# Loading the first half of an output projection in two transfers instead of one

## The chip, the core and the metric

The kernel runs on one core of a Trainium2 chip. A core has TensorE (matrix products), VectorE, ScalarE and GpSimd, which compute, and SyncE, which here issues most of the transfers. Sixteen DMA engines move data between HBM and the on-chip memory (SBUF); results of TensorE go to PSUM. The metric is the device time of one execution in microseconds (us), lower is better. The times given are of three timed runs; the profile is of one further execution.

## The reference

One token (a vector x of 1024) goes through two branches, and the results are added to it. A is attention with 32 query heads and 4 key/value heads over the last 4096 positions of a cache; B is a two-layer network with 3584 hidden units. Everything is bf16.

```python
xn = layernorm(x)
# A: attention over the last W = 4096 cached positions
q = (layernorm(x) @ wq)                      # 1024 -> 32 heads x 128
p = softmax(q k^T * 128**-0.5)               # 8 query heads share one k/v head
A = (p v).reshape(4096) @ wo                 # 4096 -> 1024
# B: network on the layernorm of xn
B = gelu(layernorm(xn) @ w1 + b1) @ w2 + b2  # 1024 -> 3584 -> 1024
out = x + A + B
```

The inputs that are read once each: the two cache windows k and v (4 MB each), wq (8 MB), w1 and w2 (7 MB each), wo (8 MB), together 39.9 MB.

## The kernel before, in words

All large inputs pass through a ring of four SBUF buffers of 32 KB in each of 128 partitions (`ring_tile`). They are loaded by SyncE in this order: k (four loads), wq in two halves, w1 in two halves, v (three loads), w2 in two halves, wo in two halves. A load into the ring waits until the buffer's earlier content has been used. The two halves of wo take the buffers of the second half of w1 and of v, so the first half of wo waits for the last matmul on w1 (L250), and the second half for the last matmul of the attention's weighted sum (`o_all`, L306). A DMA announces its landing on one of eight semaphores that are used in turn; a load on a semaphore waits for the landing of the load that used it before.

A weight matrix is laid out so that partition p holds a run of consecutive rows. For wo (4096 x 1024) that is 32 rows of 2 KB per partition, 16 in each half; "row r" below is such a slice of 128 partitions x 1024 numbers. The first half came in one load of 16 rows, a contiguous 32 KB run per partition. The second half comes in loads of 8, 4, 2, 1 and 1 rows (list `cuts`, L219).

The last stage is a product of vectors with matrices. The list `chunk_src` holds the 28 rows of w2 (kind "h", multiplied with the hidden vector `hT`) and then the 32 rows of wo (kind "o", multiplied with the attention output `o8`), in that order. For each row TensorE does two matmuls of 512 columns, one for each half of the 1024 outputs, in two column groups of the array, and adds them in PSUM in `accf` (L327). A matmul waits for the load that brought its row. The last four rows (TAIL) are split otherwise: at L331 and L332 the sum so far is copied out to `bulk`, and the last four rows go to two other PSUM tiles `acct` of 320 and 192 columns (L343). Between the second and third of them the copied sum of the 192 columns is added by a matmul with the identity (L339). VectorE then adds the 320 columns (L347), ScalarE copies the 192 (L348), and two small DMAs write the output.

TensorE runs its instructions in program order: the rows of w2, the rows of wo, then the tail.

Of the kernel before, what the change touches and what calls it, by code (L numbers as in the profile page):

```python
# [16 lines left out]
def kernel(  # L17
# [45 lines left out]
    def ring_tile(name):  # L63
        return ring.tile([P, RING_ELEMS], BF16, tag="ring", name=name, align_bytes=256)
# [151 lines left out]
        nc.sync.dma_start(out=tv, in_=w2_v[:, nr * i:nr * (i + 1), :])  # L216
        chunk_src += [("h", nr * i + r, tv[:, r, :]) for r in range(nr)]
    wo_v = A_wo.rearrange("(p c) n -> p c n", p=P)
    for i, cuts in enumerate([[0, 16], [0, 8, 12, 14, 15, 16]]):  # L219
        nr = CWO // 2  # L220
        t = ring_tile(f"wo{i}")
        tv = t[:].rearrange("p (r n) -> p r n", r=nr)
        for a, b in zip(cuts[:-1], cuts[1:]):
            nc.sync.dma_start(out=tv[:, a:b, :], in_=wo_v[:, nr * i + a:nr * i + b, :])
        chunk_src += [("o", nr * i + r, tv[:, r, :]) for r in range(nr)]
# [156 lines left out]
```

## Time and profile before

| | |
|---|---|
| three timed runs, median | 101.91 us (101.83 to 101.96) |
| profiled execution, its own time | 102.12 us |
| span of the profiled execution | 100.3 us |
| TensorE busy | 45.9 us (46%) |
| VectorE, ScalarE, GpSimd busy | 38.2, 30.0, 8.2 us |
| moved by DMA | 39.91 MB, 398 GB/s over the span |
| mean granted clock of TensorE | 0.912 |
| SyncE's queue: packets, share of 16 DMA engines' time | 2866, 93.6% |

The span goes from the first to the last instruction of the program; the time also has what lies around it. In the profile, L327 is line 327 of the kernel; "PE" is TensorE's matmuls. A line of the page with a digit for each of 40 slices gives the busy share of a slice in tenths, and "PEclk" the granted share of TensorE's clock. "From issue to landing" of a DMA counts its wait in the queue behind other loads. An arrow in the table of groups names the instruction or load that ended an idle stretch.

### The profile page before, as it was taken

What the parts mean: (1) busy time and instruction counts of PE and PEld (TensorE: products, weight loads), DVE (VectorE), ACT (ScalarE), POOL (GpSimd) and SP (SyncE); (2) the same over time, 40 slices, a digit from 0 to 9 for tenths busy, and PEclk for the clock granted to TensorE, in tenths of its full rate; (3) what the DMA queues carried; (4) which work ended last, traced back from release to release, by engine and by line L of the source; (5) the groups of instructions that cost most, each with busy time, mean ns of one, the idle gap of its engine ahead of it and who ended that gap; (6) DMA issues with size and microseconds to landing.
All of it is one profiled execution on the core that took longest, in us unless ns stands there. A gap on an engine that the chain in (4) does not pass through costs nothing.

```text
span 100.3 us, 917 instructions
## 1 busy us (share of the span) xinstructions
PE 45.9 (46%) x361; PEld 17.6 (18%) x361; DVE 38.2 (38%) x26; ACT 30.0 (30%) x35; POOL 8.2 (8%) x38
## 2 busy tenths in 40 slices
PE   0005230008500940590078721999376910299990
PEld 0002200002100300230033311344132400033330
DVE  0079999999999960000001235600600000000030
ACT  5206500007999999800000029200040000000010
POOL 7901560000000000000000001000000000000000
PEclk9999999999999999999655998599999999655998
DMA  4899999999999998998999998998999999999910
GB/s 52 372 428 427 503 470 418 457 431 418 418 418 392 469 446 366 503 400 372 413 428 421 438 510 377 492 423 372 503 400 415 418 418 431 425 421 410 399 37 1
DMA packets 2951, 39.91 MB, mean 398 GB/s; under 512 B 370, under 2 KB 388, under 8 KB 772
## 3 DMA queue, kind: packets, MB, share of 16 engines
q1 hardware_dynamic: 2866, 39.85, 93.6%
q8 instruction: 3, 0.05, 0.2%
q10 hardware_dynamic: 82, 0.01, 0.1%
HBM read 39.86 MB, written 0.00 MB: 397 GB/s over the span
## 4 chain that ended last, share of the span: by engine, by line
DMA 79%; PE 17%; DVE 0%; SPq 0%; issue 0%
DMA wo<-in_A_wo_dram 33%; DMA w<-in_B_w_dram 24%; DMA wq<-in_A_wq_dram 17%; PE accf L327 9%; DMA k_sb<-in_A_k_cache_dram 5%; PE accq L233 4%; PE acch L250 3%; PE acct L343 1%; DVE res L347 0%; PE acct L339 0%; SPq L202 0%
## 5 line engine op out<-in xcount | busy, mean ns | idle before, releaser
L195 ACT COPY kT<-kt_scr 32x4096 bf16<-32x4096 bf16 x5 | 18.0, 3601 | 10.4 <-DVE kt_scr L186 10.3
L186 DVE STREAM_TRANSPOSE kt_scr<-k_sb 128x4096 bf16<-128x4096 bf16 x4 | 17.4, 4414 | 5.7 <-DMA k_sb<-in_A_k_cache_dram 5.7
L233 PE MATMUL accq<-wq,xnT 128*1 128x512 bf16 x64 | 7.2, 626 | 15.6 <-DMA wq<-in_A_wq_dram 15.6
L197 DVE COPY kT<-kt_scr 32x4096 bf16<-32x4096 bf16 x11 | 13.4, 1218 | 0.2
L327 PE MATMUL accf<-wo,o 128*1 128x512 bf16 x56 | 9.0, 498 | 6.5 <-DMA wo<-in_A_wo_dram 6.5
L250 PE MATMUL acch<-w,yT 128*1 128x448 bf16 x64 | 6.3, 572 | 10.9 <-DMA w<-in_B_w_dram 10.9
L332 DVE COPY bulk<-accf 33x320 f32<-33x320 f32 x1 | 0.5, 483 | 23.7 <-ACT bulk L331 23.7
L306 PE MATMUL o_all<-v_sb,eTb 128*32 128x512 bf16 x32 | 8.6, 435 | 1.1 <-DVE rs L290 1.1
L259 DVE COPY qm_f<-qT_ps 128x16 bf16<-128x16 bf16 x2 | 0.3, 169 | 17.9 <-PE qT_ps L254 17.9
L331 ACT COPY bulk<-accf 33x192 f32<-33x192 f32 x1 | 0.3, 313 | 22.1 <-PE accf L327 22.1
L327 PE MATMUL accf<-w,hT 128*1 128x512 bf16 x56 | 6.4, 379 | 0.9 <-DMA w<-in_B_w_dram 0.9
L233 PEld LDWEIGHTS <-xnT 128*1 128x1 bf16 x64 | 2.1, 115 | 20.6 <-issue 19.8
L276 ACT COPY m_rep<-m_row 1x128 f32<-1x128 f32 x1 | 0.3, 297 | 16.7 <-DVE m_row L274 16.7
L327 PEld LDWEIGHTS <-o 128*1 128x1 bf16 x56 | 3.0, 104 | 12.5 <-issue 10.8
L250 PEld LDWEIGHTS <-yT 128*1 128x1 bf16 x64 | 2.1, 115 | 14.7 <-issue 14.7
L306 PEld LDWEIGHTS <-eTb 128*32 128x32 bf16 x32 | 3.4, 109 | 5.8 <-issue 1.9
L297 POOL TENSOR_SCALAR zcol<-l_loc 128x1 f32<-128x1 f32 x1 | 0.2, 238 | 46.4 <-ACT e L283 46.4
L134 PE MATMUL x_ps<-x,spread 32*128 32x8 bf16 x4 | 0.2, 163 | 7.8 <-DMA x<-in_A_x_dram 7.8
L327 PEld LDWEIGHTS <-hT 128*1 128x1 bf16 x56 | 2.4, 83 | 4.4 <-issue 1.2
L313 ACT CAST o_bf<-o_f 32x128 bf16<-32x128 f32 x1 | 0.3, 297 | 9.4 <-DVE o_f L311 9.4
L309 DVE TENSOR_TENSOR o_m<-o_all,grs 32x512 f32<-32x512 f32 x1 | 0.7, 678 | 5.9 <-PE o_all L306 5.9
L145 PE MATMUL ln_tot<-st,ones_f 128*128 128x2 f32 x4 | 1.2, 363 | 2.8 <-ACT sq L143 2.8
(81 smaller groups left out, 39.9 us busy)
## 6 DMA issues: line engine op xcount, KB each, us to landing
w<-in_B_w_dram SPq DMA_DIRECT2D x4, 3584.0 KB, 19.2
wq<-in_A_wq_dram SPq DMA_DIRECT2D x2, 4096.0 KB, 24.0
k_sb<-in_A_k_cache_dram SPq DMA_DIRECT2D x4, 1024.0 KB, 9.1
wo<-in_A_wo_dram SPq DMA_DIRECT2D x1, 4096.0 KB, 33.2
v_sb<-in_A_v_cache_dram SPq DMA_DIRECT2D x1, 2048.0 KB, 19.4
v_sb<-in_A_v_cache_dram SPq DMA_DIRECT2D x2, 1024.0 KB
wo<-in_A_wo_dram SPq DMA_DIRECT2D x1, 2048.0 KB, 20.9
wo<-in_A_wo_dram SPq DMA_DIRECT2D x1, 1024.0 KB, 23.0
```

What stands on the lines that cost most here:

```text
L145: nc.tensor.matmul(tot[:], lhsT=ones_f[:], rhs=st[:], start=True, stop=True)
L186: nc.vector.transpose(out=scr[:, g, :], in_=k2[:, g, :])
L195: nc.scalar.copy(out=dst, in_=src)
L197: nc.vector.tensor_copy(out=dst, in_=src)
L233: nc.tensor.matmul(accq[32 * t:32 * t + 1, b, :], lhsT=xnT[:, c:c + 1], rhs=w3[:, r, j * 512:(j + 1) * 512], start=(c == 0), stop=(c == C ...
L250: nc.tensor.matmul(acch[32 * t:32 * t + 1, b, :NH], lhsT=yT[:, c:c + 1], rhs=w3[:, r, j * NH:(j + 1) * NH], start=False, stop=(c == C - 1) ...
L259: nc.vector.tensor_copy(out=dst, in_=src)
L306: nc.tensor.matmul(o_all[:].rearrange("h g d -> h (g d)"), lhsT=eTb[:, 32 * c:32 * c + 32], rhs=v4[:, :, c, :], start=(c == 0), stop=(c == ...
L309: nc.vector.tensor_tensor(out=o_m[:], in0=o_all[:], in1=grs[:].unsqueeze(2).to_broadcast([Hq, Hkv, Dh]), op=ALU.mult)
L327: nc.tensor.matmul(accf[32 * half:32 * half + 1, :], lhsT=vec[kind](c), rhs=wap[:, half * 512:(half + 1) * 512], start=False, stop=(idx == ...
L332: nc.vector.tensor_copy(out=bulk[0][:], in_=accf[0:33, 0:N1])
L343: nc.tensor.matmul(t[32 * half:32 * half + 1, :], lhsT=vec[kind](c), rhs=wap[:, half * 512 + n0:half * 512 + n1], start=(idx == 0), stop=( ...
```

## The change

The list of row bounds for the first half of wo gets one more bound, 8. The loop over neighbouring bounds then issues two loads of eight rows (16 KB per partition) in place of one of sixteen (32 KB per partition), into the same buffer, one behind the other. Every other load, and each instruction of the compute engines, stays. The matmuls on rows 0 to 7 wait for the first load, those on rows 8 to 15 for the second. The loads that come after it use the next semaphore in turn.

```diff
     wo_v = A_wo.rearrange("(p c) n -> p c n", p=P)
-    for i, cuts in enumerate([[0, 16], [0, 8, 12, 14, 15, 16]]):
+    for i, cuts in enumerate([[0, 8, 16], [0, 8, 12, 14, 15, 16]]):
         nr = CWO // 2
         t = ring_tile(f"wo{i}")
         tv = t[:].rearrange("p (r n) -> p r n", r=nr)
         for a, b in zip(cuts[:-1], cuts[1:]):
             nc.sync.dma_start(out=tv[:, a:b, :], in_=wo_v[:, nr * i + a:nr * i + b, :])
         chunk_src += [("o", nr * i + r, tv[:, r, :]) for r in range(nr)]
```

## The prediction

> **What bounds the kernel now.** I read the page first for the slices over time, then the DMA issues, the chain that ended last, and last a table of stretches cut where the granted clock changes. The page's slices:
>
> ```profile
> PE   0005230008500940590078721999376910299990
> PEclk9999999999999999999655998599999999655998
> DMA  4899999999999998998999998998999999999910
> wo<-in_A_wo_dram SPq DMA_DIRECT2D x1, 4096.0 KB, 33.2
> ...
> wo<-in_A_wo_dram SPq DMA_DIRECT2D x1, 2048.0 KB, 20.9
> wo<-in_A_wo_dram SPq DMA_DIRECT2D x1, 1024.0 KB, 23.0
> ```
>
> One slice is 2.51 us. The transfers are busy from the second slice to the 38th without a hole, so loading 39.9 MB sets the length, and whatever changes only in the middle is free. The long landings (33.2 us for the first half of wo) are queueing behind earlier loads. After the 38th slice only a tail is left, and there TensorE matters. The chain that ended last:
>
> ```profile
> 53.95 33.17 DMA wo<-in_A_wo_dram
> ...
> 87.16 8.98 PE accf L327 x54
> 96.14 0.44 PE acct L343 x7
> 96.57 0.46 PE acct L339 x4
> 97.03 0.47 PE acct L343 x6
> ...
> 97.53 0.48 DVE res L347
> ```
>
> The first half of wo lands whole at 87.12. From there TensorE works without a pause to 97.5, since a backlog (16 rows) lies before it and the other half arrives meanwhile. By the landing records of the trace the later pieces arrive at 91.96 (8 rows), 94.40 (4), 95.63 (2), 96.23 and 96.85 (1 each). The last row's matmuls start at 97.18, 0.33 us after their data. So the tail of this execution is TensorE's, but with only 0.33 us over the last landing.
>
> Stretches of TensorE, cut at the trace's clock changes (the columns after the stretch and its length are busy time, granted clock, DMA share, GB/s):
>
> ```profile
> 55.26:58.67 3.41, 1.99 (x33) 1.00 1.08 458
> 58.67:62.09 3.42, 0.60 (x4) 1.00 1.10 473
> 62.09:65.50 3.41, 3.04 (x8) 0.50 0.97 420
> 79.15:82.56 3.41, 1.53 (x16) 1.00 1.07 461
> 82.56:85.98 3.42, 0.00 (x0) 1.00 0.98 422
> 85.98:89.39 3.41, 2.23 (x12) 0.50 0.97 418
> 89.39:92.81 3.42, 3.42 (x20) 0.50 0.96 405
> 92.81:96.22 3.41, 3.41 (x38) 1.00 0.77 305
> ```
>
> Every change of clock lies on a grid of 3.413 us, and the busy time of the stretch before it decides. At full clock, stretches with 1.53 and 1.99 us of work kept it, and those with 0.60 and 0.00 lost it. At half clock, 2.23 did not bring it back, while 3.04 and 3.42 did. So the idle time before 87.16 costs the clock, and the unbroken backlog that follows wins it back at 92.81, in time for the tail. This is the row on which the forecast turns. A pair of matmuls (one row of wo) takes 0.427 us at half clock and 0.2155 at full clock, by the starts of L327.
>
> **The change part by part.**
>
> *One load becomes two: the queue.* SP issues one more load at about 54.3 us. That takes 0.33 to 0.43 us of SP, which then waits until 71.06 for o_all to free the ring buffer of the next load: hidden by 16 us. The loads share eight semaphores in turn, so all later wo loads move on by one. The last row's load now follows the first w2 load on its semaphore. That one has landed by about 69 us, before the 71.06 at which the group is issued, so no wait grows. Without that cover the row's load would be late by as much as w2 were.
>
> *The transfer itself.* Packets halve from 32 KB to 16 KB. The packet records of the trace have both: 1213 ns for 32 KB (first half of wo), 611 ns for 16 KB (first piece of the second half). Eight partitions per engine took 9.681 us as 32 KB and 4.862 us as 16 KB, so two such stretches are 9.724: +0.04 us on every later landing, the last included. A gain is excluded, as the rate per packet falls with size in these records (27.0, 26.8, 26.5 GB/s per engine at 32, 16, 8 KB). The upper bound is a load that has to start up anew: the first packet of the kernel's first load came 1.04 us after its issue. I take +0.05, since the five pieces of the second half follow each other without a gap in the same records; range 0 to +1.0.
>
> By the Trainium skill, "DMA: Bandwidth & Descriptors", section on the anatomy of one DMA, a load on the GpSimd path has about 2.0 us of fixed cost that does not scale with size; unhidden, that would make the sum +2.0. The back-to-back pieces of wo in this trace do not show it.
>
> *The backlog goes.* The first eight rows land at about 82.3: 16 KB packets end 4.84 us before the others, and landing follows by the same lag. TensorE, idle since 80.69, does their 8 pairs at full clock (8 x 0.2155 = 1.72) to 84.1. The second eight land at 87.17 and are done at 88.9. The piece of 91.96 lands at 92.01, the next at 94.45. Were the clock full all along, the 4 pairs from 94.5 end at 95.4 instead of 95.97. The tail then follows its landings: the last row starts at 96.85 + 0.05 + 0.04 = 96.94 instead of 97.18. That is 0.24 us sooner, and no more can be won.
>
> *The clock in the tail.* TensorE now works in bursts of 1.72 us with idle gaps of about 3.1 us. On the grid of this execution, the stretch 82.56:85.98 holds about 1.5 us of work and 85.98:89.39 1.7, both about what kept the clock before. But 89.39:92.81 holds 0.76 us only (from 92.05). That lies between 0.60 (lost) and 1.53 (kept), far nearer to the loss, so I take the clock as lost at 92.81. Then 3.5 pairs are done by 92.81. The other 4.5 at 0.427 run to 94.73, and of the last four 3.5 are done by 96.22, where a full stretch brings the clock back. The bulk ends 0.36 us later than now (96.33 against 95.97 in starts), and the rest of the chain hangs on it: +0.36. Bounds: -0.24 if the clock is kept; if it is never brought back, the 12 pairs from 92.05 need 5.1 us, to 97.2, and the tail (0.60 + 0.49 + 0.60, partly overlapping) about 0.5 to 0.8 more: some +1.7.
>
> The grid is not tied to the kernel, so I set it at four places in turn (a boundary at 92.81, 93.66, 94.52, 95.37):
> - 92.81: as above, +0.36.
> - 93.66: 90.25:93.66 holds 1.61 us of work, the clock is kept: -0.24.
> - 94.52: 84.27:87.69 holds 0.5 us, the clock is lost at 87.69. Two half-clock stretches follow with about 2.4 and 2.5 us of work, between 2.23 (not brought back) and 3.04. If brought back, -0.24; if not, about +1.5.
> - 95.37: 88.54:91.96 holds 0.35 us, the clock is lost at 91.96, and back at 95.37 after a full stretch: 7.8 slow pairs and 4.2 fast ones end at 96.3, +0.31.
>
> The same four places for the kernel now: 0 at 92.81. At the others the backlog gets its clock back earlier or at the same pace, TensorE catches up before the last pieces, and the end lies on the landings: about -0.29.
>
> **The sum.** The profiled execution took 102.12 us (span 100.3 and 1.8 around it); the three timed runs have 101.83 to 101.96, median 101.91. That they lie 0.2 below it fits a kernel whose usual end is the landings (102.12 - 0.29 = 101.83). The four places for the changed kernel give 102.48, 101.88, 101.88 or 103.6, and 102.43. Their middle lies between 102.15 and 102.45, and I take 102.3: the tail loses about 0.4 against 101.91.
>
> **The rivals.**
> 1. *The clock is kept through the gaps.* All gaps are shorter than a grid stretch (3.1 against 3.41 us), so no stretch is wholly idle. Then the end lies on landings 0.05 later: 101.96, no change. Against it: 0.60 us of work in 58.67:62.09 did not keep the clock. The Trainium skill, "TensorE: Matmul & The Clock Gate", section "What's actually happening", says that the clock goes after at least one idle window; read strictly that is this rival, and the stretch with 0.60 us of work speaks against the strict reading.
> 2. *Faster.* The backlog is what the usual execution ends with, not only the profiled one, the 0.2 us between them being the profiler's. With the clock kept, the tail moves from TensorE to the landings: 101.91 - 0.24 = 101.67. It decides if TensorE's last row now usually starts more than 0.25 us after its landing. For it: in the one execution shown it is 0.33. Against it: it needs the clock as well.
> 3. *The second load starts up anew*, 1.04 us on every later landing: 102.95. Against it: no gap between pieces in the packet records.
>
> **How the numbers follow.** About 0.2% (0.2 us) is what a measurement can tell from no change. The forecast (clock lost in a burst, 102.3) has 0.57, rival 1 0.18, rival 2 0.20, rival 3 0.05. Slower is 0.57 + 0.05 = 0.62, same 0.18, faster 0.20. The forecast's own range is 102.1 to 102.9 by the four places. The range over all goes down to 101.75, taking in rival 1 and leaving out most of rival 2, and up to 102.9.
>
> **What the profile of the changed kernel would show.** L327 on wo in four bursts, the first from about 82.3, with idle waits on wo of some 1.6, 3.1, 3.1 us. The later landings shifted by under 0.1 us, and 16 KB packets at 611 ns. Right: a stretch at clock 0.50 that ends within or after the burst of 92.0, pairs at 0.427 us there, and L343 starting at about 96.3. Wrong: clock 1.00 from 82 to the end, with L343's last row waiting on its load. One execution shows one place of the grid, so it can end on either side; the timed runs decide. If the landing at 91.96 moves by more than 0.2 us, the transfer was mispriced.

## The result and the profile after

The changed kernel took 102.31 us (median of 22 runs, 101.87 to 103.83), the kernel before 101.91 (22 runs, 101.70 to 102.22). The ratio is 1.0039, with a 95% interval of 1.0021 to 1.0056: slower by 0.4 us, which the 0.2% limit of the prediction can still tell from no change. The longest run (103.83) is left out of the ratio.

More is to be read from the single runs than from their median. They don't lie around it: 9 of 22 are at 101.87 to 102.04, 10 at 102.23 to 102.74, and 3 at 103.14 to 103.83. The profiled execution (101.95 us, span 100.2) belongs to the first group, so by itself it shows the change at its best. TensorE in its last stage, from the timeline of the changed kernel (start, length, engine, line; in brackets the idle time before it and what ended it):

```profile
82.45 1.89 PE L327 MATMUL accf<-wo,o 128*1 128x512 bf16 x16 [0.68 <-DMA wo<-in_A_wo_dram]
87.29 3.36 PE L327 MATMUL accf<-wo,o 128*1 128x512 bf16 x16 [2.95 <-DMA wo<-in_A_wo_dram]
92.14 1.89 PE L327 MATMUL accf<-wo,o 128*1 128x512 bf16 x16 [1.48 <-DMA wo<-in_A_wo_dram]
94.58 1.03 PE L327 MATMUL accf<-wo,o 128*1 128x512 bf16 x8 [0.56 <-DMA wo<-in_A_wo_dram]
95.82 0.60 PE L343 MATMUL acct<-wo,o 128*1 128x320 bf16 x8 [0.21 <-DMA wo<-in_A_wo_dram]
```

The one run of 56 matmuls has become four bursts with gaps. The second burst, with as many matmuls as the first, took 3.36 us and not 1.89: half clock. The stretches of the clock's grid in the same execution (busy time of TensorE, granted clock, DMA share, GB/s):

```profile
80.72:84.14 3.42, 2.74 (x26) 1.00 0.96 412
84.14:87.55 3.41, 0.46 (x6) 1.00 1.04 447
87.55:90.96 3.41, 3.10 (x16) 0.50 0.96 411
90.96:94.38 3.42, 1.89 (x16) 1.00 0.98 406
```

The gap before the second burst left 0.46 us of work in one stretch, and the clock was lost at 87.55. The slow burst itself filled the next stretch with 3.10 us, and that brought it back at 90.96, before the last pieces. This is near the third place of the prediction (a boundary near 94.5), in its better outcome: the stretch after the loss holds 3.10 us, where the prediction had 2.4 and left open whether that is enough. The end of the chain:

```profile
72.39 23.39 DMA wo<-in_A_wo_dram
95.78 0.04 issue
95.82 0.60 PE acct L343 x8
96.42 0.42 PE acct L339 x4
96.84 0.52 PE acct L343 x6
97.36 0.02 issue
97.38 0.48 DVE res L347
```

The chain now leaves TensorE at 95.78 for a load, the one of the two rows before the last two, and not for the first half of wo. From here I use one number for each execution: from the landing of the last row to the start of VectorE's addition (L347). It was 0.68 us in the profile of before and is 0.38 here, the least that any profile shows: the tail waits for its data. The last row landed at 97.00.

### The profile page after: what moved, and what is told of

It reads as the page before. It is cut to its first block, busy times and chain, and to the rows that moved or that the text cites. A ratio compares the mean times of both kernels' runs of the same rounds, so it can differ in the third digit from the quotient of the medians.

```text
span 100.2 us, 918 instructions
## 1 busy us (share of the span) xinstructions
PE 47.3 (47%) x361; PEld 17.9 (18%) x361; DVE 38.2 (38%) x26; ACT 30.0 (30%) x35; POOL 8.2 (8%) x38
## 4 chain that ended last, share of the span: by engine, by line
DMA 69%; PE 21%; DVE 3%; ACT 2%; SPq 1%; issue 1%; DVEq 0%
DMA w<-in_B_w_dram 24%; DMA wo<-in_A_wo_dram 23%; DMA wq<-in_A_wq_dram 17%; PE o_all L306 10%; DMA k_sb<-in_A_k_cache_dram 5%; PE accq L233 4%; PE acch L250 3%; PE sp L267 2%; DVE eTb L286 1%; DVE m_loc L270 1%; ACT e L283 1%; PE acct L343 1%; SPq L224 1%; DVE res L347 0%; PE acct L339 0%
## 5 line engine op out<-in xcount | busy, mean ns | idle before, releaser
L250 PE MATMUL acch<-w,yT 128*1 128x448 bf16 x64 | 6.1, 562 | 11.0 <-DMA w<-in_B_w_dram 11.0
L327 PE MATMUL accf<-wo,o 128*1 128x512 bf16 x56 | 8.2, 440 | 5.7 <-DMA wo<-in_A_wo_dram 5.7
L306 PE MATMUL o_all<-v_sb,eTb 128*32 128x512 bf16 x32 | 9.6, 474 | 1.0 <-DVE rs L290 1.0
L327 PE MATMUL accf<-w,hT 128*1 128x512 bf16 x56 | 7.9, 450 | 0.0
L250 PEld LDWEIGHTS <-yT 128*1 128x1 bf16 x64 | 2.1, 116 | 14.8 <-issue 14.8
```

The source lines that it names most:

```text
L250: nc.tensor.matmul(acch[32 * t:32 * t + 1, b, :NH], lhsT=yT[:, c:c + 1], rhs=w3[:, r, j * NH:(j + 1) * NH], start=False, stop=(c == C - 1) ...
L306: nc.tensor.matmul(o_all[:].rearrange("h g d -> h (g d)"), lhsT=eTb[:, 32 * c:32 * c + 32], rhs=v4[:, :, c, :], start=(c == 0), stop=(c == ...
L327: nc.tensor.matmul(accf[32 * half:32 * half + 1, :], lhsT=vec[kind](c), rhs=wap[:, half * 512:(half + 1) * 512], start=False, stop=(idx == ...
```

## The experiments

Times are medians in us; the ratio is against the kernel before on the same chip, with its 95% interval (it is not the quotient of the two medians). "Tail" is the number just named, from the one profiled execution of each.

| kernel | time | ratio | tail |
|---|---|---|---|
| before | 101.91 | | 0.68 |
| the change | 102.31 | 1.0039 (1.0021 to 1.0056) | 0.38 |
| 1: rows 8 to 15 first | 102.11 | 1.0015 (0.9999 to 1.0031) | 0.38 |
| 2: extra pairs, misplaced | 102.38 | 1.0042 (1.0021 to 1.0063) | 0.85 |
| 3: one load, gap filled | 101.92 | 0.9997 (0.9983 to 1.0010) | 0.38 |
| 4: four and twelve rows | 102.03 | 1.0013 (0.9999 to 1.0028) | 0.38 |
| 5: extra pairs in place | 102.02 | 1.0021 (1.0012 to 1.0030) | 0.38 |
| 6: two loads, backlog, filled | 102.11 | 1.0028 (1.0018 to 1.0038) | 0.38 |
| 7: twelve and four rows | 102.04 | 1.0028 (1.0008 to 1.0048) | 0.94 |
| 8: four loads of four rows | 102.87 | 1.0103 (1.0075 to 1.0132) | 1.91 |
| 9: one load, filled in place | 101.92 | 1.0000 (0.9989 to 1.0010) | 0.39 |
| 10: 6 again, beside 9 | 102.08 | 1.0018 (1.0007 to 1.0030) | 0.38 |
| 11: v in one load | 101.93 | 1.0010 (0.9996 to 1.0024) | 0.38 |
| 12: the change again | 102.50 | 1.0044 (1.0019 to 1.0069) | 0.92 |

Two theories stood against each other. By the clock theory the change costs time because TensorE works in bursts and has half clock in the tail. By the transfer theory a second load costs it, in the queue or at landing.

**1: the same loads, but rows 8 to 15 first.** TensorE waits for the second load and has its backlog again.

```diff
-        chunk_src += [("o", nr * i + r, tv[:, r, :]) for r in range(nr)]
+        rows = list(range(8, nr)) + list(range(8)) if i == 0 else list(range(nr))
+        chunk_src += [("o", nr * i + r, tv[:, r, :]) for r in rows]
```

> Both loads stay as in the changed kernel; only TensorE's order over the first half of wo is turned, rows 8 to 15 before rows 0 to 7, so that it starts when the second load has landed and works off 16 rows without a pause, as before the change. Clock theory (the change lost its time because TensorE works in bursts and has half clock in the tail): the unbroken backlog brings the clock back, 101.9 to 102.0, with runs within about 0.5 us of each other. Transfer theory (two loads cost the time in the queue or at landing): nothing in the loads has changed, 102.3 as the changed kernel.

102.11, and no run over 102.39 where the change has 10 of 22 above that. By the ratio (1.0015 against 1.0039 and 1.0044) more than half of the loss goes away with the bursts, although the loads are the same. In its profile the clock is lost at 83.97 and the backlog, with 3.38 us of work in one stretch, brings it back at 90.80, before the tail. That speaks for the clock theory, though the intervals of the ratios overlap and this run alone does not show it. And 0.1 to 0.2 us more than expected stay, so both theories may have a part.

**2: extra matmuls in the gaps.** Into the loop over the rows, ahead of rows 28, 36 and 44 of the list:

```diff
+    scratch = ps_tp.tile([P, 512], FP32, tag="tp", name="scratch")
+    fill_before = {28: 4, 36: 8, 44: 8}
     for idx, (kind, c, wap) in enumerate(chunk_src[:n_bulk]):
+        for f in range(fill_before.get(idx, 0)):
+            for half in range(2):
+                nc.tensor.matmul(scratch[32 * half:32 * half + 1, :], lhsT=hT[:, f, 0:1],
+                                 rhs=chunk_src[f][2][:, half * 512:(half + 1) * 512],
+                                 start=True, stop=True, tile_position=(0, 32 * half))
```

> The changed kernel, and in TensorE's gaps before the three bursts on wo 4, 8 and 8 extra pairs of matmuls on rows of w2 that lie in SBUF, into a PSUM tile that nobody reads (0.9, 1.7, 1.7 us at full clock, gaps of about 1.7, 3.1, 3.1). Clock theory: no stretch is idle enough to lose the clock, the end lies on the landings, 101.85 to 101.95, runs within 0.3 us. Transfer theory: 102.3. If extra work simply delays TensorE: 102.5 or more.

102.38, like the change: by the expectation this would be a verdict for the transfers. The timeline says why it is none:

```profile
76.64 4.48 PE L330 MATMUL scratch<-w,hT 128*1 128x512 bf16 x40
80.96 3.19 PE L334 MATMUL accf<-w,hT 128*1 128x512 bf16 x28
83.98 1.89 PE L334 MATMUL accf<-wo,o 128*1 128x512 bf16 x16
87.32 1.89 PE L334 MATMUL accf<-wo,o 128*1 128x512 bf16 x16 [1.44 <-DMA wo<-in_A_wo_dram]
92.15 4.48 PE L334 MATMUL accf<-wo,o 128*1 128x512 bf16 x24 [2.95 <-DMA wo<-in_A_wo_dram]
```

All 40 extra matmuls read rows that were there early, and the program's scheduler put them ahead of the second half of w2. The gap of 2.95 us that mattered stayed open, and the burst behind it ran at half clock from 93.10 on. The stretches show the case of which the prediction's sum was made:

```profile
86.27:89.69 3.42, 1.89 (x16) 1.00 0.97 417
89.69:93.10 3.41, 0.95 (x10) 1.00 0.96 400
93.10:96.51 3.41, 3.41 (x20) 0.50 0.74 293
```

0.95 us of work in the stretch around the gap, and the clock is gone at 93.10, in the middle of the last stage.

**3: the kernel before with the gap filled.** The same lines in the kernel before, with `{28: 22}`. Here the scheduler moved some of the extra pairs too, 14 ahead of the second half of w2 and 8 behind it, but TensorE had full clock from 78.2 us to the end.

> The kernel before with its one load, and 22 extra pairs (4.7 us at full clock) in the gap of 6.5 us before the first half of wo, into a PSUM tile that nobody reads. Clock theory: the backlog of 16 rows is worked at full clock in every execution, the end lies on the landings: 101.8 to 101.85, runs within 0.3 us, and about 0.05 under the changed kernel with filled gaps, which would be the price of the second load. If the kernel before is not held by its tail at all: 101.91, no change.

101.92, the same as before (101.95 on that chip). In its profile the last row's matmuls start 0.04 us after their landing (97.17 and 97.13). So the landings are the usual end of the kernel before, and its clock was no loss that could be won back; expected was a gain of 0.1.

**4: four and twelve rows.** `[[0, 4, 16], ...]`: two loads again, but TensorE is idle for 5.6 us and then has a backlog of twelve rows.

> Two loads again, but of four and twelve rows. TensorE is left with a backlog of 12 rows at 87.2, and idle for more than 5 us before it. Clock theory: the clock is lost before the backlog, in which at half clock (12 x 0.427 = 5.1 us, up to the next landing) it is won back: 101.9 to 102.0, runs within 0.3 us. Transfer theory: as many loads and bytes as in the changed kernel, 102.3.

102.03, 1.0013 of before where the change has 1.0039 and 1.0044, with as many loads and bytes: near the expectation of the clock theory, under that of the other. As expected, the clock is lost before the backlog (at 86.95 in the profile) and won back in it (at 90.36). Again the intervals overlap.

**5: extra matmuls that can't move.** The lines of 2, but each group reads the four rows just before its gap:

```diff
+        for f in range(fill_before.get(idx, 0)):
+            fk, fc, fw = chunk_src[idx - 1 - f % 4]
+            for half in range(2):
+                nc.tensor.matmul(scratch[32 * half:32 * half + 1, :], lhsT=vec[fk](fc),
+                                 rhs=fw[:, half * 512:(half + 1) * 512],
```

> The changed kernel with filled gaps once more. In the earlier trial all 20 extra pairs ran before the second half of w2, because their data was there, and the gap of 2.95 us before the piece of 92.1 stayed open. Here each group of extra pairs (4, 8, 8) reads rows of the load that lies just before its gap, so that it can't run earlier. Clock theory: no gap over 1.5 us is left, the clock is kept to the end, and the two clusters of times of the changed kernel (101.9 to 102.0 and 102.2 to 103.8) become one: 102.0, from 101.9 to 102.2. Transfer theory, or extra work delaying TensorE: 102.3 or more.

102.02, all 12 runs between 101.92 and 102.25: one group, as expected. Stretches of this kernel:

```profile
82.92:86.33 3.41, 3.01 (x28) 1.00 1.05 452
86.33:89.74 3.41, 2.58 (x24) 1.00 1.04 447
89.74:93.16 3.42, 2.20 (x22) 1.00 0.91 377
93.16:96.57 3.41, 2.39 (x26) 1.00 0.69 274
```

The clock stays at 1.00. TensorE does more work than in the changed kernel, nobody uses it, and the runs above 102.25, more than half of the change's, are gone; the ratio falls from 1.0039 and 1.0044 to 1.0021. This is the most direct evidence for the clock theory. Yet it is still slower than before, by 0.21% (0.12 to 0.30).

**6, 9 and 10: the price of the second load by itself.** One load or two, each worked off as one backlog (with the order of 1 where there are two), with 22 extra pairs in the gap ahead of it that read rows of the second half of w2. In their profiles TensorE has full clock from 77.74 us or earlier to its last matmul.

> Two loads of eight rows, worked off as one backlog (rows 8 to 15 first) and with 22 extra pairs in the gap before it, which is the price of the second load by itself: the counterpart with one load took 0.9997 of the kernel before (0.9983 to 1.0010). If the two loads cost what their packets show (0.04 us on the landings): 101.95, 1.000 of before. If a second load costs 0.1 to 0.2 at the last landing, as the unfilled backlog (102.11) and the four-and-twelve split (102.03) may mean: 102.05 to 102.1, 1.001 to 1.0015.

> The kernel before with one load of sixteen rows and 22 extra pairs between w2 and wo, each on rows of the second half of w2, so that TensorE has no long gap there: the twin of the next kernel with one load in place of two. With the tail at full clock the end lies on the landings. Expected 0.999 to 1.000 of the kernel before, as the earlier filled one (0.9997).

> The same with two loads of eight rows, worked off as one backlog, repeated beside its twin on one chip: the difference of the two is the price of the second load without any clock effect. Packet theory (16 KB packets cost what their records show): 0.04 us more than the twin. Load theory (each further load delays the end by 0.1 to 0.25 us whatever its size): 0.1 to 0.25 us more.

Two loads: 1.0028 and 1.0018; one load: 1.0000. Side by side, 102.08 against 101.92, that is +0.16 us, with an uncertainty about as large (each ratio is good to 0.1%), but both measurements of the two loads have intervals above 1, and 6 came out over the highest of its expectations (1.0015). The packets' 0.04 was too little.

The profiles have two places where the rest may lie. The last landing is at 96.85 to 97.13 in the four profiles with one load (before, 3, 9, 11; mean 97.01), and at 96.92 to 97.25 in the nine with two (mean 97.11): +0.1, with as much scatter. The other is the end of the program: from the start of L347 to the end of the span it is 2.78, 2.78 and 2.79 us with one load (before, 3, 9), mostly 2.84 to 2.86 with two (seven profiles; the other two have 2.78 and 2.79), 2.93 with four (8), and 2.74 with two loads fewer (11). The trace's semaphore records say why: at the end SyncE waits for the semaphores one after the other in a fixed order, each step taking about 0.06 us, and stands at the one of the output's landing. With the second load SyncE's output takes the next of the eight semaphores in turn, and in this order that one stands one step earlier (the second and not the third), so that one step more lies behind it. The wait for it begins a step sooner and is longer by as much (823 ns in the kernel before, 890 in the changed one, which the view rounds):

```profile
SPq L377 <- DMA out_dram<-res: 0.8, 1, 0.8
...
SPq L377 <- DMA out_dram<-res: 0.9, 1, 0.9
```

(above before, below the changed kernel). Clearer are the records from the landing of the last output to the end of the span: 0.94 us with one load (before, 3, 9) and 1.00 in six of the nine profiles with two. In the other three (4, 6, 10) ScalarE's output landed last. Its semaphore stands at the third step, and there it is 0.93 or 0.94 again.

So 0.06 of the 0.16 us is this, in an execution in which SyncE's output lands last. About 0.1 goes with the later landing, of which the packets explain 0.04; this split is worked out from the profiles and not shown by a run of its own.

**7 and 8: other bursts.** `[[0, 12, 16], ...]` and `[[0, 4, 8, 12, 16], ...]`.

> Two loads of twelve and four rows. TensorE works without a pause from about 84.8 to 88.3 and has one gap of 3.7 us before the piece of 92.05, where the changed kernel has two of 3.1. Clock theory: the clock is lost only where a stretch falls into that one gap, and is then won back in the tail: 101.95 to 102.15 median with the slower half up to 102.6. Transfer theory: as many loads as in the changed kernel, 102.3, and the same spread.

> Four loads of four rows: bursts of 0.86 us every 2.4 us, then a gap of 3.9 us. Clock theory: a stretch of 3.41 us holds 0.9 to 1.7 us of work in the bursts and under 0.6 in the gap, so the clock is low in the tail in most executions: median 102.4 to 103.1, few runs under 102.0. Transfer theory at the 0.4 us of the changed kernel for each added load: 103.1, and a lowest run of about 102.8 too; at 0.1 us for each: 102.2, with all runs shifted alike.

Twelve and four gave 102.04, eight of twelve runs at 101.86 to 102.14 and four at 102.32 to 102.82: the times are as expected. The path to them is another in the profiled execution (102.77). The gap of 4.06 us before the first burst cost the clock at 85.89, the burst at half clock took 5.30 us and so left a gap of 1.98 in place of 3.7, and yet the clock went again at 92.72, after a stretch with 1.43 us of work. Four of four gave 102.87 (102.33 to 103.57), inside the clock theory's range; the transfer theory at 0.4 us for each load had a lowest run of 102.8. Its profiled execution had the worst tail of all, 1.91 us:

```profile
83.99:87.40 3.41, 1.17 (x10) 1.00 1.06 452
87.40:90.82 3.42, 1.63 (x8) 0.50 0.96 410
90.82:94.23 3.41, 2.13 (x12) 0.50 0.99 410
94.23:97.64 3.41, 3.41 (x22) 0.50 0.41 154
```

1.17 us of work lost the clock; 1.63 and 2.13 us did not bring it back, and so it stayed low until 97.64. Its last row landed at 97.01, no later than with two loads: the loss is TensorE's.

**11: v in one load instead of three,** in the kernel before.

```diff
-    for g0, g1 in ((0, 2), (2, 3), (3, 4)):
+    for g0, g1 in ((0, 4),):
```

> The kernel before with the cache of v in one load instead of three, same packets of 8 KB. Nothing waits for a part of it alone: it lands at about 60.4 and TensorE needs it at 62.5. Load theory: two loads fewer, 0.2 to 0.5 us less than the kernel before, 101.4 to 101.7. Packet theory: no change, within 0.1.

101.93, no gain, interval 0.9996 to 1.0024. That every load costs 0.1 to 0.25 us wherever it stands is thereby refuted; in the profile only the last 0.04 us (2.74 against 2.78) became shorter.

**12: the change again,** beside 9 and 10.

> The changed kernel as it is, again, beside its parts on the same chip. Two clusters of times as in the first series (9 of 22 at 101.87 to 102.04, the others at 102.23 to 103.83), median 102.2 to 102.5. Above the two loads without clock effect (next to it) by 0.1 to 0.4: that difference is the clock's part.

102.50 (7 runs: 101.79, 101.95, and five at 102.41 to 102.76), ratio 1.0044. Here the profile caught an execution in the second group (102.41 us):

```profile
85.20:88.62 3.42, 1.47 (x14) 1.00 1.05 450
88.62:92.03 3.41, 0.42 (x4) 1.00 0.93 396
92.03:95.44 3.41, 3.40 (x18) 0.50 0.95 383
```

The clock goes at 92.03, 0.04 us after the piece of eight rows has landed (91.99), and comes back at 95.44. The burst on the last 24 matmuls takes 4.42 us:

```profile
92.04 4.42 PE L327 MATMUL accf<-wo,o 128*1 128x512 bf16 x24 [3.00 <-DMA wo<-in_A_wo_dram]
96.29 0.60 PE L343 MATMUL acct<-wo,o 128*1 128x320 bf16 x8
...
97.28 0.60 PE L343 MATMUL acct<-wo,o 128*1 128x320 bf16 x8
```

L343 starts at 96.29 and not at 95.82 as in the first profile, though the last row landed earlier (96.92 against 97.00). This is what the prediction named as the sign of being right: half clock through the burst of 92.0 and L343 at about 96.3.

None of these kernels beats the kernel before: with one load and the clock kept (3, 9) it ends on its landings, where it ended before.

## Why the prediction was right

- *The forecast, 102.3 and slower.* Measured 102.31 and, again, 102.50. The cause it named, half clock in a burst of the tail, is shown: each profile with a tail over 0.8 us has it there (2, 7, 8, 12); with as many loads and without it (1, 4, 5) about half of the loss or more goes; made worse (8) it grows. That the median meets the forecast to 0.01 us is luck. With two runs more or fewer in the group at 101.9 the median would be about 102.1 or 102.5, and two terms of the sum are off in opposite directions, as told below under the transfer.
- *The four places of the grid* gave 102.48, 101.88, 101.88 or 103.6, and 102.43. The runs lie in three groups, at 101.9, 102.2 to 102.7 and above 103.1. The first place is the profile of experiment 2 (lost at 93.10), the third that of the changed kernel, the fourth that of experiment 12, where the prediction's 0.35 us of work before the loss was 0.42 and its "lost at 91.96, back at 95.37" was 92.03 and 95.44. The tail there was 0.92 in place of 0.38; against the profiled execution of before (0.68) that is 0.24 more, where +0.31 was worked out. These three executions took 102.63, 101.95 and 102.41 us, near the 102.48, 101.88 and 102.43 of the sum (the first has 20 extra pairs of matmuls besides). At the second place (93.66) the prediction passed over a stretch: 83.42:86.83 holds 0.68 us, less than the 0.76 that it took for a loss, so by its own rule the clock is lost there too. The burst at half clock would fill the next stretch with about 3.1 us and bring it back, so the end stays the same.
- *The bounds of the clock.* That 0.76 us, between 0.60 (lost) and 1.53 (kept), loses it was the right choice: stretches with 0.81 (7), 0.95 (2) and 1.17 us (8) lost it. Rival 1, that gaps under 3.41 us keep the clock, is refuted: gaps of 2.95 us in experiment 2 and 3.00 in experiment 12 lost it. The strict reading of the Trainium skill ("TensorE: Matmul & The Clock Gate", section "What's actually happening": at least one idle window) does not hold here, since stretches with 0.95 and 1.17 us of work lost the clock.
- *The usual end of the kernel before lies on its landings:* shown by 3 and 9 (no change with full clock, 0.9997 and 1.0000). With it falls rival 2, in which there was a gain to be had.
- *The transfer, +0.05,* is the term that was mis-sized: 0.16 to 0.25 (10 against 9; 6 against before). The packets cost what was said (611 ns each, as before). What was left out is the output's semaphore: the prediction followed the turn of the eight semaphores only to see if a load would wait, and not to the end of the program, which waits for them in order. Its own sign for a mispriced transfer, the landing at 91.96 moving by more than 0.2 us, could not see that: the landing moved by 0.13. The change's 0.4 us in the first series is so, as an estimate, about 0.2 of transfer and 0.2 of clock, where the prediction had 0.05 and 0.35; in the second series, 12 beside 10, it is 0.16 and 0.4. How large the clock's part of a median comes out depends on how many runs of a series fell on a bad place of the grid.
- *A load that starts up anew* (rival 3, +1.04) did not occur: in the two profiles of the changed kernel the later pieces landed 0.02 to 0.15 us after those of before.

## What to carry to other kernels

This kernel ends on a stream of loads, and there an earlier start of TensorE was worth nothing, since its backlog is not what usually ends last; feeding it in small bursts took away, in some executions (12), the clock with which it must run the tail. Count the busy time of TensorE in each stretch of the clock's grid around the tail, not the length of its gaps, and set the grid at several places, since one profile shows only one of them. Follow what an added load does to whatever takes turns with it, to the program's last wait.

## What the runs showed of the hardware

The clock's decision is sharper than the first profile let one see. In the 14 profiles, cut on their own grids of 3.413 us and from each execution's first clock record on, TensorE at full clock lost it after every stretch with up to 1.45 us of work and kept it after every one with 1.58 us or more; between 1.47 and 1.56 both occur. At half clock it came back after every stretch with 2.73 us or more and after none with 2.56 or less, with both between 2.68 and 2.71. In these profiles that is a share of about 45% to keep it and 79% to win it back. A stretch that is half busy therefore leaves the clock as it was, and a short burst at half clock, by lasting twice as long, may fill its stretch enough to bring the clock back, as in the profile of the changed kernel.

The clock column is to be trusted only from the first clock record on; before that it stands at 1.00. In the kernel before this record is at 45.02 us. There 32 matmuls of L250 took 3.16 us at 41.28, with 1.00 in the column, and 3.15 at 50.75, with 0.50 recorded. So the mean granted clock of 0.912, given with the time and profile before, is too high.

Not settled is why the last landing is some 0.06 us later with two loads than the packets explain. By the packet records part of it lies ahead of wo: from the mean end of w2's last sixteen packets to the last landing it is 21.04 us in the four profiles with one load and 21.10 in the nine with two. That leaves +0.06, near the packets' 0.04, and the scatter between profiles is larger than either.
